# One dealt list for the first group of a linear-attention kernel with a feed-forward block behind it

## The chip, the cores and the metric

The kernel runs on one core of a Trainium2 chip. Its engines are TensorE (PE; PEld is its weight load), VectorE (DVE), ScalarE (ACT), GpSimd (POOL) and SyncE (SP), which here issues nearly all DMAs. Each engine takes its instructions strictly in the order in which the program lists them, and waits at the head of its list for semaphores of the others. The metric is the time of one execution in microseconds, the median of several runs.

## The reference

For every batch and head (4 x 8) a state of 40 x 40 is carried through 768 steps, and the result of all heads (3072 rows of 320) goes through a feed-forward block with a gate.

```python
for t in range(S):
    y[:, :, t] = einsum('bhd,bhde->bhe', rt, state)
    Sa = einsum('bhde,bhe->bhd', state, at)
    state = state * wt - einsum('bhd,bhe->bhde', Sa, bt) + einsum('bhd,bhe->bhde', vt, kt)
x = y.transpose(0, 2, 1, 3).reshape(B * S, H * D)     # 3072 x 320
h = x @ w_in                                           # 320 x 2048
g = h * clip(h + 3, 0, 6) / 6
out = g @ w_out                                        # 2048 x 320
```

`w_in` and `w_out` arrive as 64-bit floats; the kernel makes 32-bit floats of them itself.

## The kernel before

The 768 steps are cut into blocks of 64, two at a time for two batches: 24 units, and four units (0 to 3) are a group. A unit has preparation stages (`W` and `gam`: running products of the decay by scans; `A`, `B`, `K`: transposes and scaling; `F`: the matrix to be inverted; `factor`; `E`, `EV`), and solving stages (`RT`, `VT`, `C`, `R`, `U`, `UT`, `S`, `rS`, `sn`, `H`, `y`, `move`). Between the two stands, once per group, the inversion of the group's 32 x 32 triangles, `invert` (L776): two transposes on DVE around 60 small steps, a product (L803) and a sum (L809) in turn, and then two third blocks, X and Y (`third_block`, L829), on PE and ACT, which make `tinv`. Units 0 and 2 share one state, units 1 and 3 the other. Unit 2's `R` needs the state after unit 0's `sn`.

The weights are converted in 20 pieces by the generator `load_weights` (L305). A piece is four steps: an AND on DVE with two Prelu activations on ACT behind it (L354, L355, L357), the product that finishes the piece before (L365), an AND/OR (L374), and a multiply-add (L378). The raw pieces are fetched by SP (L332) into space that is free for the moment. The 13th uses the space of the tile `x` (`raw_x`), the 14th that of `fb` (`raw_fb`), the 15th that of `tt` (`raw_tt`), both left over from the inversion; the 16th and 17th are called `raw` again. How many may be issued at all is `limit`; the token `@` in the list opens it to all 20.

The order of the instructions is written out by hand, since pools and schedule are manual. `run` lets a stage go to its next end, `aside(n)` takes n inversion steps, `deal(n)` takes n steps of the weight conversion, `fetch` (L477) has SP load an input (the stage `RT` of unit 1, 2 or 3 asks for the next unit's `R`, all of them into one tile, so that the load waits until that tile has been read), and `pieces(n)` takes n pieces of the feed-forward stream (`expand`, L1169: products `h` with `win`; `contract`, L1210: products `o` with `wout`). In the first group four lists stand one behind another: `FIRST` (preparation up to `F`), `BESIDE` (the rest of the preparation, one inversion step between stages), a loop over the remaining inversion steps with `STEPS` (at which of them a conversion step is taken, and seven early stages at every fifth), and `PLAN` (solving stages, conversion steps, feed-forward pieces, and `&`, which takes a step of the second group). From the token `&` on the same program follows for the other five groups: PE gets feed-forward pieces between the stages of units 4 to 23.

Of the kernel before, what the change touches and what calls it, by code (L numbers as in the profile page):

```python
# [12 lines left out]
AF = mybir.ActivationFunctionType  # L13
# [3 lines left out]
P = 128  # L17
BL = 64
HB = BL // 2
L = 32  # L20
# [11 lines left out]
def kernel(  # L32
# [42 lines left out]
    nc = tc.nc  # L75
    B, H, T, D = r.shape
# [3 lines left out]
    NU = 2 * NP  # L80
    DM, DFF = moe_w_in.shape
    NJ = DFF // P
    NH = NU * H
# [57 lines left out]
    def ps_pair(*dims):  # L141
# [21 lines left out]
        out=ident[:], in_=ones, pattern=[[1, P]],  # L163
# [4 lines left out]
        out=ones[:, 0:BL], in_=ones[:, 0:BL], pattern=[[1, BL]],  # L168
# [3 lines left out]
        out=ones[BL:P, 0:BL], in_=ones[BL:P, BL:P], pattern=[[1, BL]],  # L172
# [5 lines left out]
    three = const.tile([P, 1], F32, name="three")  # L178
# [59 lines left out]
    tinv = const.tile([P, NH, BL], F32, name="tinv")  # L238
# [24 lines left out]
    for i, (x, y) in enumerate([(0, DFF // 2), (0, NJ // 2)]):  # L263
        for n, z in enumerate((x, y)):
# [4 lines left out]
            name = ("WA", "BK")[i][n]  # L269
# [8 lines left out]
    converted = [0]  # L278
    phase = [0]
    limit, refill = [2], []  # L280
# [155 lines left out]
    def blocked(name, i):  # L436

        return i >= {"A": 3 * NU, "R": 2 * NU}.get(name, NK)
# [41 lines left out]
    def fetch(name, i, engine=None):  # L480

        if i is None or i >= NK:
            return
        x, crossed = {"W": (w, 0), "A": (a, 0), "B": (b, 0), "K": (k, 0), "R": (r, 1),
                      "V": (v, 1)}[name]
        if name == "V":
            t = values[i % AHEAD]
        else:
            t = placed.get((name, i))
            if (name, i) == ("R", 1):  # L490
                t = others["K"]
            t = t if t is not None else (others if i < 2 * NU and i % 2 and name != "R" else inputs)[name]
        g, p = names[i]
        if blocked(name, i):
            t = fetch_blocks(name, x, 2 * p, g, i == (2 * NU if crossed else 3 * NU))
            data[i][name + "N"] = t
            return
        engines = engine or nc.sync
        for q in range(2):
            engine = engines[q] if isinstance(engines, tuple) else engines  # L500
            y = x[2 * p + q, :, g * BL:(g + 1) * BL, :]
            rows = slice(q * BL, (q + 1) * BL)
            if crossed:
                for s in range(2):
                    engine.dma_start(out=t[rows, 4 * s:4 * s + 4, 0:D],  # L505
                                     in_=y[s::2].rearrange("h t e -> t h e"))
            else:
                engine.dma_start(out=t[rows, :, 0:D], in_=y.rearrange("h t e -> t h e"))  # L508
        data[i][name + "N"] = t
# [254 lines left out]
    def in_turn(stages, order):  # L764

        for name in order:
            yield from stages[name]()
            shared[0] = None
            yield DONE
# [107 lines left out]
    def third_blocks(first=False):  # L877

        zs = inv.tile([P, 2, 2, H, L], F32, name="zs", tag="x", bufs=1)
        return [third_block(*third[-1], 2 * n, zs[:, n], first) for n in range(2)]  # L880
# [359 lines left out]
    weights = load_weights()  # L1240
# [11 lines left out]
    def aside(n, weight=0):  # L1252

        for _ in range(n):
            if side and next(side[0], side) is side:
                side.popleft()
            due[0] += weight
            while due[0] >= 1:
                due[0] -= 1
                next(weights, None)  # L1260

    def deal(n):

        for _ in range(n):
            next(weights, None)

    def run(stage, steps=0, mixed=0, deals=0):

        for at in stage:
            if at == DONE:  # L1270
                return
            aside(steps, mixed)
            deal(deals)

    third, F, group_F = [], None, []

    def prepared(i):
        nonlocal F
        if i >= NK:
            return None  # L1280
        if i % NU == 0:
            F = inv.tile([P, NH, BL], F32, name="F", tag="F", bufs=2)
            group_F.append(F)
        return prepare(i, F)
# [3 lines left out]
    EARLY, MIXED, MOVED = 5, 0.27, 2  # L1288
# [23 lines left out]
    begin = [prepared(i) for i in range(NU)]  # L1312
    for group, first in ("WAB", 0), ("WAB", 2), ("K", 0), ("V", 0), ("K", 2), ("V", 2):
        if (group, first) == ("V", 2):
            next(weights)
        for name in group:
            for i in range(first, first + 2):
                fetch(name, i, (nc.sync, nc.scalar) if first == 0 and name != "V" else None)
    FIRST = "0W 1W 0gam 1gam 0A 1A 2W 3W 0B 1B 0F 1F 2gam 3gam 2A 3A 2B 3B 2F 3F".split()
    BESIDE = "2K 1K 1factor 0K 3K 0factor 2factor 0E 3factor 1E 2E 0EV 3E 3EV 2EV 1EV".split()  # L1320
    chains = [in_turn(begin[i], [x[1:] for x in FIRST + BESIDE if x[0] == str(i)]) for i in range(NU)]
    for x in FIRST:
        run(chains[int(x[0])])
# [3 lines left out]
                        (SLOT, 6 * D, SLOT + 8, L), (SLOT, 6 * D + BL, SLOT + 8, L)):  # L1327
        nc.gpsimd.tensor_copy(select[x:x + D, at:at + n], ident[x:x + D, c:c + n])
    side.append(invert(group_F[-1], third, True))
    for n, x in enumerate(BESIDE):  # L1330
        limit[0] = {0: 4, 8: 12}.get(n, limit[0])
        while n == 0 and refill[0]():
            pass
        if n == 4:
            fetch("R", 0)
            fetch("R", 1)
        run(chains[int(x[0])], 1, MIXED if n >= 12 else 0)
    TURNS_IN = [("one", 1), ("pair", 2), ("pair", 2)]
    blocks = {}


    stages = [step(i) for i in range(NU)]
    chains = [in_turn(stages[0], ["RT", "VT", "C", "R"]), in_turn(stages[1], ["RT", "VT", "C"])]
    early = deque(chains[i] for i in (0, 0, 1, 1, 0, 1, 0))
    STEPS = (4, 12, 13, 27, 29, 31, 35, 37, 55, 58, 62, 64, 67)
    n, cleared = 0, []
    while not third:
        aside(1)
        if not third:
            n += 1  # L1350
            if n in STEPS:
                next(weights, None)
            if converted[0] >= 2 and not cleared:
                cleared.append(True)
                for z in range(0, P, BL):
                    nc.scalar.activation(out=tinv[z + L:z + BL, :, 0:L], func=AF.Copy, scale=0.0,
                                         in_=_ap(three[z + L:z + BL], 0, [[0, NH], [0, L]]))
            if n % EARLY == 0 and early:
                run(early.popleft())
    assert not early and cleared  # L1360
    limit[0] = 13
    while phase[0] == 1:
        next(weights)
    firsts = third_blocks(True)

    def block(i, j):

        if i % NU < 2:
            if j == 0:
# [3 lines left out]

    PLAN = """X:2 X 0U:4 +1 0UT:1 0sn:2 1R 0H:1 1U 1UT:2
              0y 1sn:1 0move:1 Y:2 2RT:1 1H:1 Y:1 2VT:3 1y:2 2R
              2S:3 2U:3 1move:1 3RT:2 ! @ 2UT 2C:3 2rS:3 3R:4
              *2 3VT 3S:1 2sn:3 *1.5 2H:6 *3 3U:1 # 3UT:7
              2y:3 +8 +1 +2 +2 +1 +1 +3 +1 +2  # L1380
              +2 +4 3C:6 +1 +4 +2 +3 +3 +3 +2
              +5 +4 +3 +1 +2 +4 +1 +5 & +1
              +4 +2 +3 +4 +1 +3 +4 3rS:13 +5 +2
              +1 +3 +3 +4 +3 +3 3sn +2 +4 +1
              +1 +2 +1 +2 +2 +2 +1 +1 3H:8 +4
              +4 & +2 +6 +1 +1 +1 +6 +3 +1
              +3 +4 +2 +6 +4 % +3 +1 +3 +2
              +1 +2 +2 +1 +3 *2.5 +4 2move:8 *1.5 +2
              +1 +3 +2 & +2 +3 2move2:17 +5 3y:4 +4
              & +1 +3 3move:5 +1 +3 +1 +3 +2 +1  # L1390
              +2 +1 +4 & +3 3move2:1 +4 +2 & +2
              +2 +3 +2 +4"""
    chains = {str(i): in_turn(stages[i], [x[1:].split(":")[0] for x in PLAN.split() if x[0] == str(i)])
              for i in range(NU)}
    chains.update({x: firsts[n] for n, x in enumerate("XY")})
    for x in PLAN.split():
        if x == "!":
            begun_ffn()
            ring.clear()
            ring.extend([("one", 1), ("whole", 2)])  # L1400
        elif x == "@":
            limit[0] = PIECES
        elif x == "#":
            seconds()
            for name in "WA":
                fetch(name, NU + 1)
            third.clear()
            second_group = by_twos(NU, 3, 0, 1.25)
        elif x == "%":
            for name in "BK":  # L1410
                others[name] = second(name)
                fetch(name, NU + 1)
        elif x == "&":
            next(second_group)
        elif x[0] == "*":
            pieces(float(x[1:]))
        elif x[0] == "+":
            deal(int(x))
        else:
            name, *amounts = x.split(":")  # L1420
            run(chains[name[0]], 0, 0, *map(int, amounts))
    for _ in weights:
        pass
    for _ in second_group:
# [94 lines left out]
    m = 0  # L1519
# [54 lines left out]
```

## Time and profile before

| what | us |
|---|---|
| median of 3 runs (786.43, 787.64, 795.53) | 787.64 |
| profiled execution, as timed | 790.31 |
| its span in the profile | 788.6 |
| PE busy in the span (91%) | 721.2 |
| DVE busy (64%) | 506.9 |
| ACT busy (38%) | 299.9 |
| POOL busy (21%) | 168.9 |
| mean granted clock of TensorE, share of full speed | 0.954 |

The span is one execution as the hardware profiler saw it; 1.7 us of the timed 790.31 lie around it. Busy shares are averages over the whole span. In a timeline row the first number is the start in the span, the second the length; then follow engine, line, operation, and what is written from what. A wait is put down to the instruction that came last before the waiting one could go.

### The profile page before, as it was taken

The page shows a single profiled execution, that of the slowest core. Times are in us where ns is not written, and L with a number is a line of the kernel's source. Part 1 is how long each engine was busy: PE and PEld are TensorE (multiplying, and loading weights), DVE is VectorE, ACT ScalarE, POOL GpSimd, SP SyncE. Part 2 cuts the span into 40 slices and gives each one's busy share as a digit, 9 for nine tenths or more (in the row PEclk, how much of TensorE's full clock was granted, in tenths as well). Part 3 has the DMA queues.
Part 4 walks back from the last instruction along what each step waited for, and adds up shares of the span by engine and source line. Part 5 has one row for each costly group of instructions (what it writes and reads, how often), then busy time and mean ns, then how long its engine had stood idle before and what let it go on. Part 6 is the DMA issues. An engine that isn't in the chain of part 4 may idle for free.

```text
span 788.6 us, 32724 instructions
## 1 busy us (share of the span) xinstructions
PE 721.2 (91%) x14456; PEld 610.9 (77%) x14456; DVE 506.9 (64%) x1018; ACT 299.9 (38%) x634; POOL 168.9 (21%) x319
## 2 busy tenths in 40 slices
PE   5736968999899898999999999999999999999998
PEld 3625757878779786888788878888888888888886
DVE  7898869789455799455899355997635982233110
ACT  2345853321554442443324454134543242422111
POOL 7503002420232412122203222203212120000000
PEclk9755789999999999899999999999999999999999
DMA  9672374330233431343322343313332101111000
GB/s 124 120 199 83 75 194 73 66 56 9 52 72 71 89 69 29 69 87 80 66 58 48 66 83 84 75 35 68 72 71 57 38 18 45 41 38 28 20 9 17
DMA packets 195698, 52.34 MB, mean 66 GB/s; under 512 B 179428, under 2 KB 194276, under 8 KB 195556
## 3 DMA queue, kind: packets, MB, share of 16 engines
q1 hardware_dynamic: 187932, 46.88, 30.0%
q10 hardware_dynamic: 7624, 3.36, 1.7%
q8 instruction: 114, 1.87, 1.0%
q14 instruction: 28, 0.23, 0.1%
HBM read 38.67 MB, written 3.93 MB: 54 GB/s over the span
## 4 chain that ended last, share of the span: by engine, by line
PE 72%; DVE 12%; ACT 4%; issue 4%; SPq 3%; DMA 3%; ACTq 1%; POOL 0%; DVEq 0%; POOLq 0%
PE h L1169 26%; PE o L1210 23%; PE pair L562 4%; PE pair L1043 3%; DVE x L809 2%; DVE prod L803 2%; PE pair L534 2%; SPq L508 2%; PE pair L961 2%; PE one L524 1%; PE pair L981 1%; PE pair L997 1%; PE pair L921 1%; PE pair L861 1%; SPq L505 1%
## 5 line engine op out<-in xcount | busy, mean ns | idle before, releaser
L1169 PE MATMUL h<-xt,win 128*128 128x128 f32 (+1 forms) x2304 | 249.7, 283 | 2.6 <-DVE gt L1185 2.6
L1169 PEld LDWEIGHTS h<-xt,win 128*128 128x128 f32 (+1 forms) x2304 | 231.0, 192 | 18.7 <-DVE gt L1185 3.3
L1210 PE MATMUL o<-wout,gt 128*128 128x320 f32 x768 | 227.3, 441 | 0.0
L1210 PEld LDWEIGHTS o<-wout,gt 128*128 128x128 f32 x768 | 138.9, 190 | 51.6
L1185 DVE SCALAR_TENSOR_TENSOR gt<-gt,h 128x512 f32<-128x512 f32 x96 | 61.9, 682 | 103.0 <-ACT gt L1184 102.8
L1184 ACT ACTIVATE gt<-h,three 128x512 f32<-128x512 f32 x96 | 62.0, 685 | 120.9 <-PE h L1169 101.6
L809 DVE TENSOR_TENSOR x<-x,prod 128x30 f32<-128x30 f32 (+9 forms) x180 | 65.1, 361 | 5.8
L803 DVE TENSOR_TENSOR prod<-x 128x30 f32<-128x30 f32 (+9 forms) x180 | 64.6, 359 | 6.5 <-POOL x L788 1.3
L575 DVE COPY_PREDICATED store<-mask,pair 128x512 f32<-128x512 int32 x40 | 29.2, 731 | 53.1 <-PE pair L562 37.8
L723 POOL TENSOR_TENSOR KBt<-K,rgt 128x320 f32<-128x320 f32 x19 | 16.6, 872 | 163.7 <-ACT rgt L712 163.6
L1051 POOL TENSOR_TENSOR yg<-ys,gam 128x512 f32<-128x512 f32 x20 | 25.4, 1270 | 115.9 <-DVE ys L1050 84.2
L599 DVE TENSOR_TENSOR_SCAN prods<-wm,start 128x528 f32<-128x528 f32 x24 | 33.5, 1402 | 12.2 <-ACT wm L596 11.8
L1043 PE MATMUL pair<-store,KBt 64*64 64x104 f32 x1280 | 32.6, 250 | 0.7 <-ACT F L693 0.5
L757 ACT ACTIVATE EV<-pair 64x320 f32<-64x320 f32 x44 | 18.9, 431 | 37.0 <-PE pair L752 33.5
L610 DVE TENSOR_TENSOR_SCAN wm<-wm,start 128x528 f32<-128x528 f32 x24 | 31.0, 1291 | 0.8
L1043 PEld LDWEIGHTS pair<-store,KBt 64*64 64x64 f32 x1280 | 29.2, 133 | 1.4 <-ACT F L693 0.7
L738 DVE TENSOR_TENSOR kt<-pair,rgam 128x512 f32<-128x512 f32 x15 | 10.3, 685 | 30.0 <-PE pair L703 29.6
L642 POOL TENSOR_TENSOR at<-at,gam 128x512 f32<-128x512 f32 x12 | 15.3, 1272 | 57.7 <-DVE at L478 51.9
L1228 ACT ACTIVATE ob<-o 128x320 f32<-128x320 f32 x22 | 9.6, 437 | 46.0 <-issue 26.3
L965 ACT ACTIVATE store<-pair 128x320 f32<-128x320 f32 x23 | 10.0, 435 | 42.2 <-PE pair L981 31.5
L950 ACT ACTIVATE S<-pair 128x512 f32<-128x512 f32 x16 | 9.6, 597 | 43.4 <-DVE store L575 23.6
L871 ACT ACTIVATE tinv<-pair 32x256 f32<-32x256 f32 x48 | 17.9, 373 | 16.4 <-PE pair L861 13.3
(306 smaller groups left out, 1069.9 us busy)
## 6 DMA issues: line engine op xcount, KB each, us to landing
R<-in_r_dram SPq DMA_DIRECT2D x156, 40.0 KB
A<-in_a_dram SPq DMA_DIRECT2D x61, 80.0 KB
V<-in_v_dram SPq DMA_DIRECT2D x96, 40.0 KB
out_dram<-ob SPq DMA_DIRECT2D x47, 80.0 KB
B<-in_b_dram SPq DMA_DIRECT2D x42, 80.0 KB
store<-V SPq DMA_DIRECT2D x20, 160.0 KB
W<-in_w_dram SPq DMA_DIRECT2D x37, 80.0 KB
K<-in_k_dram SPq DMA_DIRECT2D x37, 80.0 KB
```

The costliest lines, as they stand in the source:

```text
L562: nc.tensor.matmul(out=o[i][half(q), n, :], lhsT=lhs[half(i, D), n ^ (2 * q * swap), half(q)], rhs=rhs[half(i, D), n ^ (2 * q * back), hal ...
L575: nc.vector.copy_predicated(out=x[:, :, 0:BL].rearrange("p (h i) t -> p i h t", i=2), mask=mask8, data=o[2])
L599: nc.vector.tensor_tensor_scan(out=prods[:].rearrange("p r m i -> p (r m i)"), data0=wm[:, 0:SCAN], data1=start[:], initial=0.0, op0=ALU.m ...
L610: nc.vector.tensor_tensor_scan(out=back, data0=back, data1=start[:], initial=0.0, op0=ALU.mult, op1=ALU.add)
L803: nc.vector.tensor_tensor(out=pv, in0=_ap(x[:], (i + 1) * L + i, [[L, n], [0, i]]), in1=_ap(x[:], i * L, [[0, n], [1, i]]), op=ALU.mult,)
L809: nc.vector.tensor_tensor(out=rest, in0=rest, in1=pv, op=ALU.add)
L1043: nc.tensor.matmul(out=y[q][half(s), pr, :], lhsT=o[name][half(q), h * D:h * D + SLOT], rhs=m[name][half(q), x, :], start=(name == "K" and ...
L1051: nc.gpsimd.tensor_tensor(out=yg[:], in0=m["ys"][:].rearrange("p r q t -> p r (q t)"), in1=o["G"][:], op=ALU.mult)
L1169: nc.tensor.matmul(out=hp[c][:, i, :], lhsT=lhsT, rhs=rhs, start=(begun[c] == 0), stop=(begun[c] == 3 * NQ - 1))
L1184: nc.scalar.activation(out=gt[:], in_=hp[c][:], func=AF.Relu, bias=three[:], scale=1.0)
L1185: nc.vector.scalar_tensor_tensor(out=gt[:], in0=gt[:], scalar=6.0, in1=hp[c][:], op0=ALU.min, op1=ALU.mult)
L1210: nc.tensor.matmul(out=op[:], lhsT=gts[c][:, n, :], rhs=wout[:, c * HJ + r * NQ + n, :], start=((split or r == 0) and c == 0 and n == 0), ...
```

## The change

The three lists behind `FIRST` become one `PLAN`, and some orders in it are new. New tokens: `i` or `m` behind a stage's number takes an inversion step at its inner stop (`m` with a share of a conversion step), `=n` takes n inversion steps, `Ln` sets `limit`, `<` fetches raw pieces, `r` fetches `R` of units 0 and 1, `z` clears a part of `tinv`, `T` takes what is left of the inversion and makes X and Y. `+n`, `*n`, `!`, `@`, `#`, `%` and `&` are what they were, and the feed-forward pieces in the list add up to 10.5 in both.

```diff
-    FIRST = "0W 1W 0gam 1gam 0A 1A 2W 3W 0B 1B 0F 1F 2gam 3gam 2A 3A 2B 3B 2F 3F".split()
-    BESIDE = "2K 1K 1factor 0K 3K 0factor 2factor 0E 3factor 1E 2E 0EV 3E 3EV 2EV 1EV".split()
+    FIRST = "0W 0gam 1W 1gam 0A 1A 2W 3W 0B 1B 0F 1F 2gam 3gam 2A 2B 3A 3B 2F 3F".split()
+    BESIDE = "0K 1K 1factor 0factor 2K 2factor 0E 3K 2E 3factor 1E 0EV 2EV 1EV 3E 3EV".split()
...
-    for n, x in enumerate(BESIDE):
...
-        run(chains[int(x[0])], 1, MIXED if n >= 12 else 0)
...
-    early = deque(chains[i] for i in (0, 0, 1, 1, 0, 1, 0))
-    STEPS = (4, 12, 13, 27, 29, 31, 35, 37, 55, 58, 62, 64, 67)
-    while not third:
-        aside(1)
...
-    PLAN = """X:2 X 0U:4 +1 0UT:1 0sn:2 1R 0H:1 1U 1UT:2
-              0y 1sn:1 0move:1 Y:2 2RT:1 1H:1 Y:1 2VT:3 1y:2 2R
-              2S:3 2U:3 1move:1 3RT:2 ! @ 2UT 2C:3 2rS:3 3R:4
-              *2 3VT 3S:1 2sn:3 *1.5 2H:6 *3 3U:1 # 3UT:7
-              2y:3 +8 +1 +2 +2 +1 +1 +3 +1 +2
-              +2 +4 3C:6 +1 +4 +2 +3 +3 +3 +2
-              +5 +4 +3 +1 +2 +4 +1 +5 & +1
...
+    PLAN = """1K:0i L4 < 1factor:0i r 0K:0i 0factor:0i 2K:0m 2factor:0i 0E:0i
+              3K:0i 2E:0i =1 1E:0i 2EV:0m 1EV:0m =5 L12 3factor:0i =4
+              0EV:0i 3E:0m 3EV:0m 0RT =2 +1 =1 =4 +1 0VT
+              =4 =4 =1 1RT =1 +1 +1 =2 +1 =3
+              1VT +1 =4 0C +1 =1 =2 1C =1 =1
+              +1 =2 +1 z =4 =2 =2 =11 =1 +1
+              T 0R:1 X X:2 0U:4 0UT 0sn:2 1R:2 +1 1U
+              0H:1 1UT:2 1sn:1 0y 2RT:1 Y:2 0move:1 1H:1 Y:1 2VT:3
+              1y:1 2R 2S:4 @ 1move 3RT:2 2U:3 ! 2UT 2C:3
+              *1.5 2rS:3 3R:4 3VT:1 # *2 2sn:2 3S:1 2H:6 *3
+              3U:1 3UT:7 2y:4 +1 3C:3 +2 & 3rS:11 3sn:1 *2.5
+              3H:8 & % *1.5 2move:6 & 2move2:15 3y:4 & 3move:4
+              & 3move2:3 &"""
...
+        elif x == "T":
+            while not third:
+                aside(1)
+            limit[0] = max(13, limit[0])
+            while phase[0] == 1:
+                next(weights)
+            chains.update({x: x_chain for x, x_chain in zip("XY", third_blocks(True))})
+        elif x[0] == "=":
+            for _ in range(int(x[1:])):
+                if not third:
+                    aside(1)
```

Instruction by instruction, none is added or taken away. On PE, DVE, ACT and POOL the two programs differ in order up to the beginning of the second group only, and so do SP's loads.

More of the change, by code (lines that the diff above doesn't have):

```diff
@@ L1329 @@
     side.append(invert(group_F[-1], third, True))
-    for n, x in enumerate(BESIDE):
[L1331 to L1336, printed above, removed]
-        run(chains[int(x[0])], 1, MIXED if n >= 12 else 0)
     TURNS_IN = [("one", 1), ("pair", 2), ("pair", 2)]
     blocks = {}
-    stages = [step(i) for i in range(NU)]
-    chains = [in_turn(stages[0], ["RT", "VT", "C", "R"]), in_turn(stages[1], ["RT", "VT", "C"])]
-    early = deque(chains[i] for i in (0, 0, 1, 1, 0, 1, 0))
-    STEPS = (4, 12, 13, 27, 29, 31, 35, 37, 55, 58, 62, 64, 67)
-    n, cleared = 0, []
-    while not third:
-        aside(1)
[L1349 to L1364, printed above, removed]
+    stages = [{**begin[i], **step(i)} for i in range(NU)]
     def block(i, j):
@@ L1372, in block @@
             run(blocks[i])
-    PLAN = """X:2 X 0U:4 +1 0UT:1 0sn:2 1R 0H:1 1U 1UT:2
-              0y 1sn:1 0move:1 Y:2 2RT:1 1H:1 Y:1 2VT:3 1y:2 2R
-              2S:3 2U:3 1move:1 3RT:2 ! @ 2UT 2C:3 2rS:3 3R:4
-              *2 3VT 3S:1 2sn:3 *1.5 2H:6 *3 3U:1 # 3UT:7
-              2y:3 +8 +1 +2 +2 +1 +1 +3 +1 +2
-              +2 +4 3C:6 +1 +4 +2 +3 +3 +3 +2
-              +5 +4 +3 +1 +2 +4 +1 +5 & +1
[L1383 to L1392, printed above, removed]
+    PLAN = """1K:0i L4 < 1factor:0i r 0K:0i 0factor:0i 2K:0m 2factor:0i 0E:0i
[7 more added lines that the diff above has]
+              1y:1 2R 2S:4 @ 1move 3RT:2 2U:3 ! 2UT 2C:3
+              *1.5 2rS:3 3R:4 3VT:1 # *2 2sn:2 3S:1 2H:6 *3
+              3U:1 3UT:7 2y:4 +1 3C:3 +2 & 3rS:11 3sn:1 *2.5
+              3H:8 & % *1.5 2move:6 & 2move2:15 3y:4 & 3move:4
+              & 3move2:3 &"""
     chains = {str(i): in_turn(stages[i], [x[1:].split(":")[0] for x in PLAN.split() if x[0] == str(i)])
               for i in range(NU)}
-    chains.update({x: firsts[n] for n, x in enumerate("XY")})
     for x in PLAN.split():
@@ L1400 @@
             ring.extend([("one", 1), ("whole", 2)])
+        elif x[0] == "L":
+            limit[0] = int(x[1:])
+        elif x == "<":
+            while refill[0]():
+                pass
+        elif x == "r":
+            fetch("R", 0)
+            fetch("R", 1)
+        elif x == "z":
+            assert converted[0] >= 2
+            for z in range(0, P, BL):
+                nc.scalar.activation(out=tinv[z + L:z + BL, :, 0:L], func=AF.Copy, scale=0.0,
+                                     in_=_ap(three[z + L:z + BL], 0, [[0, NH], [0, L]]))
+        elif x == "T":
[9 more added lines that the diff above has]
+                    aside(1)
         elif x == "@":
@@ L1420 @@
             name, *amounts = x.split(":")
-            run(chains[name[0]], 0, 0, *map(int, amounts))
+            between = amounts[0][-1] if amounts and amounts[0][-1] in "im" else ""
+            deals = int(amounts[0].rstrip("im")) if amounts else 0
+            run(chains[name[0]], int(between != ""), MIXED if between == "m" else 0, deals)
     for _ in weights:
```

## The prediction

> **What bounds it now.** I began with the page: engines, then the forty slices (19.7 us each).
>
> ```profile
> PE 721.2 (91%) x14456; PEld 610.9 (77%) x14456; DVE 506.9 (64%) x1018; ACT 299.9 (38%) x634; POOL 168.9 (21%) x319
> ...
> PE   5736968999899898999999999999999999999998
> ...
> DVE  7898869789455799455899355997635982233110
> ...
> PEclk9755789999999999899999999999999999999999
> ```
>
> From the seventh slice on PE is busy eight to nine tenths or more at nearly full clock: the feed-forward products fill it, its order there stays, and what comes earlier shifts all of it. PE idles most in the first six slices, some 120 us (45 of them), and there DVE is the fullest engine. That is where the change works. Its instructions are the same in number, so no term below is work; each is a wait or an order. Next came the waits of DVE and of PE, 60 to 126 us (us in total, times, longest):
>
> ```profile
> DVE parts L354 <- DMA raw_fb<-in_moe_w_in_dram: 4.5, 1, 4.5
> DVE gt L1185 <- ACT gt L1184: 2.2, 1, 2.2
> DVE yg L1073 <- PE lent L1065: 2.1, 1, 2.1
> DVE yg L1073 <- PE pair L1065: 1.6, 1, 1.6
> ```
>
> ```profile
> PE pair L1015 <- DVE RR L925: 5.0, 1, 5.0
> ```
>
> One cause stands behind the largest wait on both engines. DVE reaches the AND of the 14th raw piece at 99.2 and gets it at 103.7; unit 3's `RR` (L925) stands two instructions behind it, and PE's `sn` of unit 2 (L1015) needs the bank that this empties. Why the piece is late, SP's timeline tells (start, length):
>
> ```profile
> 83.69 1.90 SPq L332 DMA_DIRECT2D raw_x<-in_moe_w_in_dram  x2
> 85.64 11.54 SPq L505 DMA_DIRECT2D R<-in_r_dram  x8
> 97.22 1.06 SPq L332 DMA_DIRECT2D raw_fb<-in_moe_w_in_dram  x2
> 98.32 2.98 SPq L332 DMA_DIRECT2D raw_tt<-in_moe_w_in_dram  x4
> ```
>
> Eight loads of `R` are issued in 11.5 us, where eight of `V` take 6.1 (row at 16.24). Four are unit 3's; the other four, unit 4's, wait for PE to read unit 3's tile, transposed from 93.5 to 94.4. `raw_fb` stands behind them in SP's list, while nothing moves (GB/s is the last column):
>
> ```profile
> 90.00:95.00 5.00, 4.99 (x76) 4.24 (x72) 4.79 (x11) 4.57 (x8) 0.00 (x0) 0.60 0.00 2
> 95.00:100.00 5.00, 4.70 (x120) 4.34 (x120) 4.14 (x9) 3.86 (x6) 0.00 (x0) 1.00 0.53 123
> 100.00:105.00 5.00, 0.21 (x2) 0.00 (x0) 1.31 (x3) 0.81 (x2) 0.17 (x1) 0.93 0.91 244
> 105.00:110.00 5.00, 4.82 (x104) 4.52 (x104) 4.93 (x11) 3.90 (x7) 0.28 (x2) 0.50 0.59 175
> ```
>
> PE's five empty microseconds (first column pair) are followed by five at clock 0.50 (third from the end).
>
> **The parts.**
>
> *Preparation (`FIRST`).* DVE idles 0.8 us at 7.6 for ACT's `wm` of unit 1. In the new order unit 0's L608 and L610 fill that, but ACT now copies unit 0's `gam` and `rgam` ahead of `wm`: two copies end some 0.75 us after L610, then `wm` takes 0.67, so DVE idles about 1.4 before unit 1's scan. Unit 0's `at` starts at 13.55 instead of 13.28. Later unit 2's `bt` goes ahead of unit 3's `at`, so that the first `F` product is done while DVE makes the rest, and only unit 3's product (0.9) and its copy (0.6) stand behind the last `bt`. That gives back up to 0.3. Sum: between -0.3 and +1.4 (nothing given back), taken as 0, since two independent shifts of 0.3 stand against each other.
>
> *Beside the inversion.* From 26 to 64 us DVE runs without a gap. Before the end of the inversion it does the same four `kt`, six masks and 60 steps, and one conversion step more, an AND/OR: +0.35 by its pitch (0.34 to 0.45). The stages that change place there are on PE and ACT, both mostly idle: their cover is the inversion itself (PE waits 11.8 us for it). Unit 2's `E` and `EV` now need `V` of unit 2 first; those loads are issued from 28.3 to about 31.5 and stay where they are. The fetch of `R` is asked for sooner, but SP issues back to back until 56 and keeps this order: 0.
>
> *The first third blocks.* ACT's timeline:
>
> ```profile
> 64.69 1.56 ACT L846 ACTIVATE zs<-lent 32x256 f32<-32x256 f32 x4 [3.69 <-DVE tt L817]
> 67.39 1.56 ACT L871 ACTIVATE tinv<-pair 32x256 f32<-32x256 f32 x4 [1.15 <-PE pair L861]
> 68.97 0.72 ACT L355 ACTIVATE parts<-parts,low 128x512 f32<-128x512 int32 x1
> 69.73 0.72 ACT L357 ACTIVATE parts<-parts,low 128x512 int32<-128x512 f32 x1
> 70.47 0.44 ACT L965 ACTIVATE store<-pair 128x320 f32<-128x320 f32 x1
> 70.81 0.71 ACT L355 ACTIVATE parts<-parts,low 128x512 f32<-128x512 int32 x1
> 71.55 0.72 ACT L357 ACTIVATE parts<-parts,low 128x512 int32<-128x512 f32 x1
> 72.18 0.58 ACT L987 ACTIVATE UT<-lent 128x512 f32<-128x512 f32 x1
> ```
>
> A pair of activations (1.45) moves into the gap of 1.15 ahead of L871, which is then some 0.3 late, and none stands between L965 and L987 any more (1.37). L965 comes about 0.2 later, `UT` 0.8 sooner: -0.8 + 0.35 = about -0.4 for `UT`.
>
> *Stages of units 1 to 3.* Now unit 1's `U` stands ahead of unit 0's `H` on PE (it waits for `RR`, 0.46 behind `UT` on ACT; a product at half clock is 1.1), unit 0's `y` behind unit 1's `sn`, and `move` of unit 0 behind Y's first product. `y` and `move` come 2 us later; they lead to `xt`, which PE first needs at 97. On the other side Y's first product stands at 80 in both, and `xt` of unit 0 and a conversion pair no longer share ACT with its copies in the old order: `tinv` is complete 0.7 sooner. Unit 2's `U`, which stood ahead of `move` of unit 1 (3.0 at low clock) and unit 3's `RT` (0.9), stands behind both. Before, its result was held on ACT from 90.8 to 93.7 by `S` and four conversion activations, so that the new place costs the path little: PE reaches `rS` of unit 2 at about 95.6 (now 95.7). DVE saves its wait for `y` of unit 1 (2.1) in part. Walked through by rows, DVE comes to the AND of the 14th piece at about 98.2 instead of 99.2. Bounds: +2 (all of `y`'s delay on the path) and -3 (both `yg` waits, 3.7, less the 0.35 and 0.3 above); I take -1.
>
> *`@` ahead of unit 3's `RT`.* It opens the last seven pieces before the load of unit 4's `R` is listed. SP can then issue `raw_fb` behind unit 3's `R`, at about 88.3 instead of 97.2, and `raw_tt` behind it. By its old times (issued 97.2, used 103.7) it has landed by 94.9, ahead of 98.2: the wait of 4.5 goes. Behind it in SP's list are `raw_tt` (before: 98.3 to use 106.2, 7.9 us; after: 89.4 to 100.5), then the first `raw`; the second `raw` now waits behind unit 4's `R`, issued at about 97 and used at 108: 11 us, where 102 to 114.8 was enough. Unit 4's `R` itself is used only in the second group. `#` ahead puts the loads of `W` and `A` before the 18th and 19th piece; 2.6 us of issue (four at 0.65), against 9.5 us between issue and use of `raw_fb`'s second piece: hidden; uncovered it would cost 2.6. If the 14th piece landed late all the same, the whole 4.5 would stay. Taken: -4.5.
>
> *After it.* With the gap gone, PE's `sn` follows its `h` products with no half clock, and DVE's 2.2 us for `gt` (L1185) shrinks, as PE finishes `h` sooner. From 0 to -3 (2.2 of `gt`, and half of the 1.5 that PE then waits for it); I take -1. The feed-forward pieces, 10.5 in sum, only change places.
>
> [...] The row is the clock 0.50 from 105 to 110 behind an idle 5.0. [...]
>
> **Sum.** 0 + 0 (the 0.35 is in the -1) - 1 - 4.5 - 1 = -6.5 at the start of the second group. I keep -6, since later waits of PE from 125 to 330 us (2.7, 1.8, 1.6 and less) may take up some. The profiled execution goes from 790.3 to 784.3; the median of the runs, 787.64, is 2.7 below that one, so the forecast is 781.6.
>
> **Rivals.** *Part is taken back* (chance 0.2): another wait is late next, such as DVE's for `sn` and `H` of unit 2, whose `U` now stands behind two stages. For it: three of the four waits above are of DVE for PE. Against: unit 2's `U` had been held on ACT anyway. Gain 4.5 + 1 - 3.5 = 2: 785.6.
>
> *PE sets the pace* (0.08): the clock stays up from 95 on, the `gt` waits vanish, and both `yg` waits: 4.5 + 3 + 3 = 10.5: 777.1. [...] Against it is DVE's row at 105, full.
>
> *Slower: unit 2's `U` waits for a load* (0.1). It used to be independent of unit 3's `R`; now it is queued on PE behind its transposes, and with it `UT`, `sn`, `H`. That `R` is issued behind `raw_x`, which waits for Y's last product to read `x`'s space. PE comes to the transposes at about 91.5; the loads end their issue at 88.2 and an `R` load lands in 2 to 3 us (2.25 at 246.67). If Y slips, each microsecond beyond 1 is a wait. A slip of 6 outweighs the gain, and at 8 it is 2 slower than before: 789.6. Against: Y comes at 80 by my walk.
>
> *It doesn't do what it says* (0.02): SP's list could keep `raw_fb` behind the `R` loads. In the built lists it stands ahead of unit 4's.
>
> **How the numbers follow.** The forecast has 0.6 (776 to 785). The range leaves out about 2 in 10: from 777 (-10.5, the fast rival's end) to 789 (+1.4, the preparation's upper bound with nothing gained, most of the slow rival outside). Two per cent is 15.8 us, about what a measurement can tell from no change. Faster by that would need more than all bounds together (3 + 4.5 + 3): 0.02. Slower by it would need a slip of Y by 22: 0.03. Within: 0.95.
>
> **What would show it.** `raw_fb` issued near 88, no wait of L354 for it, no PE gap near 100 and no clock of 0.5 behind it; `UT` near 71.8; the first `W` transposes of the second group near 113 instead of 119.9, and the rest shifted as a block. A wait of PE for `R` near 91, or of DVE for L1015 or L562 near 100, would prove me wrong; so would a shift at 120 that is gone by 200.

## The result, and the profile after

| 22 runs each | median us | lowest to highest |
|---|---|---|
| before | 787.78 | 783.1 to 796.51 |
| changed | 784.40 | 779.0 to 788.55 |

The ratio is 0.9956 (95% interval 0.9936 to 0.9976): a small gain that is there, 3.4 us by the medians, far inside the 2% that count as the same. The profiled execution took 784.76 us (span 783.0), 5.55 less than that of before.

The engines and the forty slices (19.6 us each) of the changed kernel's page:

```profile
PE 720.2 (92%) x14456; PEld 608.6 (78%) x14456; DVE 507.0 (65%) x1018; ACT 300.0 (38%) x634; POOL 169.8 (22%) x319
...
PE   5745879999899998999999999999999999999998
...
DVE  7898798688446798445998455996635982323110
...
PEclk9855899999999998899999999999999999999999
```

Busy times are the same to 1 us (PEld, which overlaps PE, to 2.3). In the sixth and seventh slice (98 to 137 us) PE's digits go from 6, 8 to 7, 9, and in the fifth and sixth its clock's from 7, 8 to 8, 9.

SP's timeline of the changed kernel shows the one moved load that the prediction counted on (start, length):

```profile
84.21 3.20 SPq L505 DMA_DIRECT2D R<-in_r_dram  x4
87.51 1.01 SPq L332 DMA_DIRECT2D raw_fb<-in_moe_w_in_dram  x2
88.57 3.17 SPq L332 DMA_DIRECT2D raw_tt<-in_moe_w_in_dram  x4
91.83 0.39 SPq L332 DMA_DIRECT2D raw<-in_moe_w_out_dram  x1
93.12 3.24 SPq L505 DMA_DIRECT2D R<-in_r_dram  x4
```

The eight loads of `R` are now two times four, and `raw_fb` goes between them at 87.51 instead of 97.22. DVE's timeline at that piece:

```profile
99.01 0.69 DVE L378 SCALAR_TENSOR_TENSOR raw_x<-raw_x 128x512 f32<-128x512 uint32 x1
99.62 0.42 DVE L354 TENSOR_SCALAR parts<-raw_fb 128x512 uint32<-128x512 uint32 x1
...
100.56 0.48 DVE L925 TENSOR_TENSOR RR<-pair,EV 128x320 f32<-128x320 f32 x1
```

No row carries an idle time in brackets: the AND of the 14th piece starts when DVE comes to it. What is left in the waits from 60 to 126 us (us in total, times, longest):

```profile
DVE yg L1073 <- PE lent L1065: 3.7, 2, 2.7
...
DVE state L1022 <- PE pair L1015: 1.6, 1, 1.6
```

The 4.5 for `raw_fb`, the 2.2 for `gt` and PE's 5.0 for `RR` are gone. Both waits for `y` are still there, 3.7 as before. The windows in which PE had stood still for five microseconds:

```profile
90.00:95.00 5.00, 4.40 (x78) 3.72 (x76) 4.90 (x11) 3.99 (x7) 0.00 (x0) 0.73 0.89 244
95.00:100.00 5.00, 4.37 (x118) 4.14 (x119) 4.88 (x12) 4.29 (x8) 0.00 (x0) 1.00 0.58 148
100.00:105.00 5.00, 4.51 (x120) 3.92 (x120) 4.93 (x12) 3.90 (x8) 0.45 (x2) 1.00 0.44 74
105.00:110.00 5.00, 3.00 (x88) 2.68 (x86) 4.93 (x10) 3.77 (x6) 0.00 (x0) 1.00 0.71 209
```

The column of the clock (third from the end) reads 1.00 from 95 on, and DVE (third pair) is busy 4.88 to 4.93 of 5: behind the 14th piece DVE sets the pace now, without a break. The first `W` transposes of the second group come at 113.44 instead of 119.87. I call this place W below; it is the mark by which the first group can be compared apart from all that follows.

### The profile page after: what moved, and what is told of

It reads as the page before. It is cut to its first block, busy times and chain, and to the rows that moved or that the text cites. A ratio compares the mean times of both kernels' runs of the same rounds, so it can differ in the third digit from the quotient of the medians.

```text
span 783.0 us, 32729 instructions
## 1 busy us (share of the span) xinstructions
PE 720.2 (92%) x14456; PEld 608.6 (78%) x14456; DVE 507.0 (65%) x1018; ACT 300.0 (38%) x634; POOL 169.8 (22%) x319
## 4 chain that ended last, share of the span: by engine, by line
PE 72%; DVE 13%; issue 4%; SPq 4%; ACT 3%; DMA 3%; POOL 0%; ACTq 0%; DVEq 0%; POOLq 0%
PE h L1169 26%; PE o L1210 23%; PE pair L562 4%; PE pair L1043 3%; PE pair L534 2%; SPq L508 2%; DVE x L809 2%; DVE prod L803 2%; PE pair L961 1%; PE pair L752 1%; PE one L524 1%; PE pair L921 1%; PE pair L997 1%; PE pair L981 1%; SPq L505 1%
## 5 line engine op out<-in xcount | busy, mean ns | idle before, releaser
L809 DVE TENSOR_TENSOR x<-x,prod 128x30 f32<-128x30 f32 (+9 forms) x180 | 65.9, 366 | 6.0
L562 PE MATMUL pair<-RT,VT 40*64 40x64 f32 x768 | 18.2, 236 | 7.6 <-ACT VT L932 3.6
```

The costliest lines, as they stand in the source:

```text
L562: nc.tensor.matmul(out=o[i][half(q), n, :], lhsT=lhs[half(i, D), n ^ (2 * q * swap), half(q)], rhs=rhs[half(i, D), n ^ (2 * q * back), hal ...
L809: nc.vector.tensor_tensor(out=rest, in0=rest, in1=pv, op=ALU.add)
```

## The experiments

Two theories stood against each other: that the place of `@`, which changes nothing but SP's list, carries the gain; and that the new dealing of steps and stages carries it. All kernels compute everything. Every time stands beside runs of the kernel before on the same chip.

| kernel | median us | before there | ratio, 95% interval | W |
|---|---|---|---|---|
| before (two traces) | | | | 119.87, 119.99 |
| changed (three traces) | 784.40 / 784.84 / 784.06 | 787.78 / 790.81 / 790.43 | 0.9956 / 0.9934 / 0.9927 | 113.44, 113.13, 112.66 |
| e1_at | 785.86 | 791.04 | 0.9947 (0.9910 to 0.9984) | 112.58 |
| e2_noat | 786.97 | 791.04 | 0.9945 (0.9915 to 0.9975) | 115.42 |
| e5_tail | 793.20 | 791.04 | 1.0032 (1.0002 to 1.0062) | 120.62 |
| e6_front | 794.73 | 791.04 | 1.0045 (1.0023 to 1.0067) | 119.81 |
| e7_tail_phase | 785.48 | 790.81 | 0.9945 (0.9920 to 0.9971) | 112.41 |
| e8_y | 784.71 | 790.81 | 0.9941 (0.9914 to 0.9967) | 112.24 |
| e9_fill | 784.87 | 789.69 | 0.9947 (0.9922 to 0.9972) | 112.35 |
| e10_afterfill | 782.15 | 789.69 | 0.9909 (0.9878 to 0.9940) | 113.54 |
| e11_fill_later | 783.60 | 790.43 | 0.9924 (0.9895 to 0.9953) | 112.81 |

### `@` alone, and everything but `@`

e1_at is the kernel before with one token moved:

```diff
-              2S:3 2U:3 1move:1 3RT:2 ! @ 2UT 2C:3 2rS:3 3R:4
+              2S:3 @ 2U:3 1move:1 3RT:2 ! 2UT 2C:3 2rS:3 3R:4
```

> The kernel before with one token moved: the permission for the last seven raw pieces stands ahead of unit 2's U instead of behind unit 3's RT, so that the 14th piece's loads are listed ahead of unit 4's R on SP. The other engines keep their lists. If that order is what the gain is made of (theory 1): no wait of DVE for the 14th piece (4.5 us before), no 5.0 us gap of PE near 100, the first W transposes of the second group 4 to 5 us sooner than 119.9, and 3 to 4.5 us faster in time. If the other moves of the dealt list carry it (theory 2): the wait goes, but another takes its place; W moves by under 1.5 us and the time by under 1 us.

Measured: `raw_fb` issued at 88.43, its AND at 98.47 without a wait, W at 112.58: 7.3 us sooner than in before (4 to 5 were expected), as much as the whole change reaches in the best of its three traces. The time is 0.9947 of before. One moved token in SP's list is enough for all of the gain.

e2_noat is the changed kernel with that token put back:

```diff
-              1y:1 2R 2S:4 @ 1move 3RT:2 2U:3 ! 2UT 2C:3
+              1y:1 2R 2S:4 1move 3RT:2 @ 2U:3 ! 2UT 2C:3
```

> The changed kernel with the same token put back behind unit 3's RT; only SP's list differs from the changed kernel. Theory 1: the 14th piece is issued near 96 again, DVE waits 3.5 to 5 us for it, and 3 to 5 us of the gain are lost, so that the time is within 1 us of the kernel before. Theory 2: at most 1.5 us are lost, it stays 2 us or more faster than before.

Measured: the loads are back in the old order, but the wait is not. SP's timeline and, below it, DVE's in that kernel:

```profile
84.23 10.95 SPq L505 DMA_DIRECT2D R<-in_r_dram  x8
95.24 1.06 SPq L332 DMA_DIRECT2D raw_fb<-in_moe_w_in_dram  x2
```

```profile
99.93 0.43 DVE L354 TENSOR_SCALAR parts<-raw_fb 128x512 uint32<-128x512 uint32 x1 [1.22 <-DMA raw_fb<-in_moe_w_in_dram]
```

`raw_fb` is issued 2 us sooner than in before, is there 4.7 us later (6.5 in before: 97.22 to 103.69), and the wait is 1.2, with 0.7 more for `raw_tt`, instead of 4.5. W comes at 115.42. So in the old list the early `@` is sufficient, and in the new one it is not necessary. Without it the new list still brings 4.45 at W; with it, 2 more. Why `raw_fb` is issued sooner can be read in the list, where unit 3's `RT`, which frees the tile of `R`, now stands ahead of unit 2's `U`: its transposes (L524) start at 91.40 instead of 93.50. Why `raw_fb` lands faster stays open.

### The two halves

e5_tail has the lists of before up to the end of the inversion, and the changed `PLAN` behind it; e6_front the other way round.

```diff
-    PLAN = """X:2 X 0U:4 +1 0UT:1 0sn:2 1R 0H:1 1U 1UT:2
+    PLAN = """X X:2 0U:4 0UT 0sn:2 1R:2 +1 1U
...
```

> The three lists up to the end of the inversion as they were before; the solving list behind it as changed. In the changed kernel the inversion ends 0.95 us later than before (61.8 against 60.8). Theory 1: this part costs what it is late, so that here the inversion ends near 60.8 again, W stands 0.5 to 1 us sooner than the changed kernel's 113.4, and the time is 0.3 to 1 us better than the changed kernel's, 4 to 4.5 us under before. Rival: the conversion step taken early in the front pays for its lateness; then W is no sooner than 113.4.

```diff
-              T 0R:1 X X:2 0U:4 0UT 0sn:2 1R:2 +1 1U
+              T 0R:1 X:2 X 0U:4 +1 0UT:1 0sn:2 1R 0H:1 1U 1UT:2
...
```

> The complement: the front as changed, the solving list as before, with the 14th piece behind unit 4's R. Theory 1: the wait for the 14th piece stays (3 to 5 us), the inversion ends 0.95 us later, W stands at 119.5 to 121, the time is 0 to 1 us above before. Rival (the front carries a part of the gain): 1 us or more under before.

Measured: neither half gains; both are slower than before, 1.0032 and 1.0045, with both intervals clear of 1. For e5_tail both forecasts failed. `raw_fb` is issued at 87.02 and there is no wait for it, and W is at 120.62 all the same: with the early `@` in place the gain can still be lost. The inversion (L812), which was to end near 60.8 again, ended at 61.73. In e6_front, which has the late `@`, W is at 119.81, as forecast, but the time is 3.7 us above before and not 0 to 1, the wait for `raw_fb` is 1.15 and not 3 to 5, and PE's wait L861 for `zs` is 5.3 us (1.9 in before). What the halves have in common is that the conversion steps, which both lists count on from wherever the front left them, stand two places off the stages that they were dealt between. In before and in the changed kernel 19 conversion steps come on DVE ahead of unit 0's `sn` (L1022); in e5_tail it is 17, in e6_front 21.

### Two steps

e7_tail_phase tests that. It is e5_tail with two conversion steps more behind the inversion (`+1`, and one more inside `X`), so that 19 come ahead of unit 0's `sn` again and every engine's order from there on is that of the changed kernel:

```diff
-    PLAN = """X X:2 0U:4 0UT 0sn:2 1R:2 +1 1U
+    PLAN = """+1 X X:3 0U:4 0UT 0sn:2 1R:2 +1 1U
```

> Like the tail alone (front as before, solving list as changed), but with one conversion step taken at once behind the inversion and one more in X, so that every engine's list behind the inversion is the changed kernel's. If the tail alone was slow only because its conversion steps fell one step off their places: W of the second group near 113.4 (120.6 without the step), time 0.993 to 0.998 of before. If the changed front is needed for something else (early state, fetches, clock): it stays at 1.000 or above and W at 117 or later.

Measured: W at 112.41 instead of 120.62, ratio 0.9945 instead of 1.0032. The expectation speaks of one step; the lists differ by two. An AND/OR and a multiply-add (L374, 0.42, and L378, 0.69) that DVE takes ahead of `sn` instead of behind it, with all later steps two places sooner, are worth 8 us. The windows of e5_tail (us; busy PE, PEld, DVE, ACT, POOL; clock, DMA share, GB/s):

```profile
76.00:90.00 14.00, 12.01 (x436) 10.65 (x428) 9.74 (x19) 10.54 (x20) 0.00 (x0) 0.74 0.57 142
90.00:105.00 15.00, 12.25 (x206) 11.20 (x204) 12.95 (x27) 10.00 (x18) 0.62 (x2) 0.73 0.56 140
105.00:121.00 16.00, 11.93 (x299) 10.67 (x299) 12.10 (x24) 9.17 (x15) 0.00 (x0) 0.77 0.47 121
```

and those of e7_tail_phase:

```profile
76.00:90.00 14.00, 11.02 (x443) 9.70 (x432) 11.46 (x23) 10.85 (x22) 0.00 (x0) 1.00 0.57 137
90.00:105.00 15.00, 11.86 (x317) 10.13 (x315) 14.59 (x31) 12.81 (x22) 0.45 (x2) 1.00 0.80 182
105.00:113.00 8.00, 4.63 (x173) 4.17 (x174) 7.90 (x16) 6.48 (x11) 0.00 (x0) 1.00 0.58 171
```

PE's clock is about three quarters in all windows of the one and full in all of the other. DVE, which has the most to do here, is busy 12.95 and 12.10 in the one, 14.59 of 15 and 7.90 of 8 in the other: at the low clock it waits for PE at `sn` (L1022, 4.4 us instead of 2.0), at `yg` and at L571, and PE waits for it in turn. How much of the 8 us the waits cost by themselves, and how much the low clock, these two runs don't separate. They do show that the front of the change (`FIRST`, `BESIDE` and the steps of the inversion) gives nothing: with the old front and the fitting steps, W is as early as in the changed kernel. It is so although the inversion ended at 62.40 in e7_tail_phase, later than in any other trace here: how early the inversion ends does not decide W.

### The waits for `y`

The waits for `y` of units 0 and 1 had outlived the change. e8_y is e1_at with a conversion step moved ahead of the first, and two ahead of the second; only DVE's order differs from e1_at.

```diff
-              0y 1sn:1 0move:1 Y:2 2RT:1 1H:1 Y:1 2VT:3 1y:2 2R
-              2S:3 @ 2U:3 1move:1 3RT:2 ! 2UT 2C:3 2rS:3 3R:4
+              0y:1 1sn 0move:1 Y:2 2RT:1 1H:1 Y:1 2VT:3 1y:4 2R
+              2S:1 @ 2U:3 1move:1 3RT:2 ! 2UT 2C:3 2rS:3 3R:4
```

> The kernel with the moved token alone, and on DVE one conversion step ahead of each of the two products of unit 0's and unit 1's y; no other engine's list changes. If DVE's waits for y (1.7 and 1.3 us there) are on the path: they shrink by 1 us or more together, W stands near 111.8 instead of 112.6, and it is 0.5 to 1 us faster than the kernel with the token alone, the fastest of all. Rival: PE's wait behind y sets the end anyway, and RR of unit 2, later on DVE by the step, costs what is gained: no change within 0.5 us.

(The expectation counts one step for each `y`.) Measured: the waits shrink from 3.0 (1.7 and 1.3 in e1_at) to 1.2, and W comes only 0.3 sooner, at 112.24, which is less than the traces of one unaltered program differ by (113.44, 113.13, 112.66). DVE's waits for PE at L1022 grow from 0.3 to 1.1 at the same time. So most of a removed wait is late at the next one; my 3.7 of `yg` waits were never worth 3.7. The ratio, 0.9941, can't be told from those of e1_at and of the changed kernel, though its profiled span was 778.6, the shortest of all.

### The same program twice

That span asked how far one trace carries. So both kernels were profiled again unaltered.

> The kernel before once more, unaltered, for the same comparison. The order on SP makes the 14th piece late again: DVE waits 3 to 5 us for it and PE 3 to 5 us near 100. If that wait is as short as in the changed kernel with the token put back (1.2), the 4.5 us were chance and not the order.

> The changed kernel once more, unaltered, to see what differs between two executions of one program. [...] Time 0.994 to 0.998 of before.

Measured: before took 790.48 (span 788.8 against 788.6) and shows the wait for `raw_fb` again, 4.7. The changed kernel took 784.84 as median and 785.6 in its profiled run. In the two traces of the changed kernel the start of the second group agrees within 0.3 us, but not what follows: from the end of the third group's inversion (L812) to the sum of its `y` (L1050) the one takes 29.62 us, the other 28.74. The kernels above take 26.8 (e2, e8), 26.9 (e5), 28.6 (e6), 29.0 (e7) and 29.5 (e1) for the same instructions. PE stands still for 2.6 us at L838 in that stretch in all of them, and then has a stretch of half clock of changing length (3.4 to 10.2 us). That is a third theory, about the part behind the change: what happens to a shift of 6 us on its way to the end would be decided by how the clock falls behind such gaps.

### Filling the gap behind

To fill that gap, e10_afterfill moves two feed-forward pieces in the changed kernel, e9_fill the same two in e8_y (the digits are pieces between blocks of the other groups, the second list those of them that come first, the third inversion steps beside each):

```diff
-    GAPS = "71042423221267761421...
-    FIRSTS = "50021102120130201200...
-    INVERSION = "01210000000015231100...
+    GAPS = "71042423221267743421...
+    FIRSTS = "50021102120130203200...
+    INVERSION = "01210000000015241100...
```

> The changed kernel with one thing moved, behind the first group: two feed-forward pieces (1.16 us each on PE) of the 16th place between blocks go to the 17th, ahead of the third group's third blocks (L838), where PE waits 2.6 us for the end of the inversion; of 18 inversion steps dealt beside them 16 stay and 2 move with the pieces. Clock theory (the 2.6 us idle lets the clock fall, and which window it falls in decides how long the stretch behind it takes): the idle of L838 near 305 goes to under 1 us, no window between 300 and 330 has a clock under 0.9, the same work from the end of the inversion (L812 of the third group) to L1050 takes 26.5 to 27.5 us instead of 28.7 and 29.6 in two traces of the changed kernel, and the time is 1.5 to 2.5 us less: 782.5 to 783.5, 0.2 to 0.3% under the changed kernel. Rival (DVE and the inversion set the pace there, the clock only follows): the idle stays as long because the inversion ends 2 us later, or moves to the place that gave the pieces up; clock and time as before, 784.8.

> The same two pieces moved in the kernel that has of the change only the place of `@` and one conversion step ahead of the `y` of unit 0 and one of unit 1 (its trace already caught the good phase there: 26.8 us at clock 0.94, span 778.6, while its median was 784.7). Clock theory: its profile gains at most 0.5 us against that trace, its median 1 to 2.5 us, and its runs spread less, since fewer of them fall into a long stretch of half clock. Rival: median 784.7 and the same spread.

Measured: the gap stays at 2.68 us in both. My design was wrong: the two pieces had stood ahead of the gap already, so that PE had no more to do there than before. That it is a window that decides how long the half clock lasts was my guess; no run here shows it. The stretch takes 26.95 and 26.83. e9_fill has the median of e8_y, 784.87; e10_afterfill has the lowest of all, 782.15, but I found nothing in its trace that explains it, and its interval overlaps those of the unaltered changed kernel.

e11_fill_later takes the two pieces from behind the gap instead. DVE's, POOL's and SP's orders are those of the changed kernel, which ran beside it on the same chip.

```diff
-    GAPS = "71042423221267761421...
-    FIRSTS = "50021102120130201200...
+    GAPS = "71042423221267763311...
+    FIRSTS = "50021102120130203200...
```

> The changed kernel; two `h` pieces (1.16 us each on PE) that stood behind the third group's first third block (L838) are done ahead of it, where PE waits 2.62 us for DVE; the two pieces before this one had been moved from ahead of the same wait and could not fill it. DVE's, POOL's and SP's lists are the same. Clock theory: the idle ahead of L838 shrinks to 0.3 to 0.5 us, no window between 305 and 335 has a clock under 0.9 (0.50 and 0.71 at 310 and 315 in the trace of the changed kernel), from the end of the inversion (L812 of the third group) to L1050 goes from 29.6 and 28.7 to 25.5 to 27 us, and the time from 784.8 to 782 to 783, beside the same kernel unaltered on the same chip 0.997. Rival: the stretch is set by DVE, or L861 and L871 now wait in place of L838, and length and time stay: 784.8, 1.000.

> The changed kernel unaltered, for the comparison with the one run beside it: 784.8. By the clock theory its trace has the idle of 2.6 us ahead of L838 near 305 and at least one window of clock 0.85 or less within 10 us behind it, but takes anything from 26.8 to 29.6 us from the end of the inversion to L1050, as the same program did before (29.6 and 28.7).

Measured: the gap ahead of L838 on PE's timeline (idle time in brackets), first in the first trace of the changed kernel, and then its windows from 305 to 320,

```profile
307.89 1.08 PE L838 MATMUL pair<-tb,F 32*32 32x32 f32 x64 [2.62 <-DVE state L1055]
```

```profile
305.00:310.00 5.00, 2.38 (x77) 2.15 (x77) 4.84 (x10) 2.70 (x8) 2.98 (x6) 0.77 0.30 65
310.00:315.00 5.00, 5.00 (x96) 4.80 (x95) 3.17 (x10) 1.19 (x3) 0.34 (x2) 0.50 0.43 91
315.00:320.00 5.00, 5.00 (x87) 4.52 (x86) 1.09 (x2) 1.45 (x4) 1.32 (x2) 0.71 0.35 80
```

then the same windows of the same program in its third trace, where the gap is again 2.62,

```profile
305.00:310.00 5.00, 2.85 (x84) 2.82 (x86) 4.88 (x8) 2.57 (x8) 2.68 (x5) 0.75 0.34 76
310.00:315.00 5.00, 5.00 (x164) 4.67 (x161) 3.56 (x9) 0.79 (x2) 0.99 (x1) 0.91 0.40 85
315.00:320.00 5.00, 5.00 (x144) 4.08 (x143) 1.28 (x2) 4.42 (x11) 0.34 (x2) 1.00 0.36 82
```

and e11_fill_later:

```profile
308.21 0.74 PE L838 MATMUL pair<-tb,F 32*32 32x32 f32 x64 [0.85 <-DVE state L1055]
```

```profile
305.00:310.00 5.00, 4.15 (x102) 3.80 (x100) 4.86 (x9) 3.03 (x8) 2.98 (x5) 1.00 0.25 58
310.00:315.00 5.00, 4.55 (x158) 3.82 (x156) 4.57 (x11) 1.72 (x4) 1.41 (x4) 1.00 0.48 101
315.00:320.00 5.00, 4.75 (x149) 3.65 (x138) 1.28 (x2) 3.58 (x10) 0.59 (x2) 1.00 0.37 82
```

With 2.62 of idle the same program gets 0.50 and 0.71 once, and 0.91 and 1.00 another time. With 0.85 the clock stays at 1.00. The stretch to L1050 takes 29.62, 28.74 and 26.81 us in the three traces of the changed kernel, and 25.93 in e11_fill_later. That half of the theory holds. The other half, that the time falls by 2 to 3 us, does not: 783.60 against 784.06 beside it, 0.9924 and 0.9927 of before. Half a microsecond is less than the medians of the unaltered changed kernel differ by (784.06 to 784.84), so these runs show no gain from this one place.

## Why the prediction was right, and where it was not

**The place of `@`, -4.5: right, in each detail.** Issue at 88.3 forecast, 87.5 measured; the wait of L354 gone, PE's 5.0 at L1015 gone, `raw_tt` and the later pieces covered. The runs add that the old order costs what it costs only in the old list: e2_noat pays 1.9 for it. The prediction put the term down to one edit; it belongs to the order of `R`, `raw_fb` and DVE's list together.

**Preparation, 0: right.** DVE's wait for `wm` is 1.19 (forecast 1.4), and the end of `FIRST`, L783, comes at 26.05 instead of 26.19.

**Beside the inversion, +0.35: too small.** It ended 0.95 later (61.80 against 60.84). The conversion step more is there. What I had not seen is unit 3's `KBt` on POOL, which comes later in the new order and beside other instructions. POOL's timeline and DVE's, of the changed kernel:

```profile
39.03 1.79 POOL L723 TENSOR_TENSOR KBt<-wout,rgt 128x320 f32<-128x320 f32 x2 [3.76 <-ACT rgt L715]
```

```profile
38.72 0.37 DVE L803 TENSOR_TENSOR prod<-x 128x198 f32<-128x198 f32 x1
39.12 0.99 DVE L809 TENSOR_TENSOR x<-x,prod 128x198 f32<-128x198 f32 x1
40.14 0.92 DVE L803 TENSOR_TENSOR prod<-x 128x210 f32<-128x210 f32 x1
41.09 0.38 DVE L809 TENSOR_TENSOR x<-x,prod 128x210 f32<-128x210 f32 x1
```

Two steps that take 0.36 and 0.38 in before (at 40.80 and 41.19) take 0.99 and 0.92 here. In before that `KBt` ran from 35.37 to 37.10, beside a mask (L571, 0.73, as long as elsewhere) and two smaller steps, of which one was stretched (L809, 0.83 at 36.42). Over the inversion the sixty steps add up to 22.9 us instead of 22.3. In these rows the two steps beside `KBt` are stretched to about the length of one of POOL's two instructions (1.79 for both); why they are, no run here shows.

**First third blocks, `UT` at 71.8: 72.16.** That is 0.36 later than forecast, less than the inversion's extra 0.6, and 0.02 ahead of before.

**The walk through units 1 to 3, -1: wrong.** DVE came to the AND of the 14th piece at 99.62, 0.45 later than before; the other two traces of the changed kernel have 99.31 and 98.84, against 99.17 and 99.29 in the two of before: about where it was. Both `yg` waits stayed (3.7), where I had let the second one shrink in part, and 0.6 of the miss is the inversion. The step of the walk that failed is the one on `y` and `move` of unit 0: they come 2 us later and lead to `xt`, "which PE first needs at 97". PE needs it at 83.3. ACT comes to that `xt` (L1095) at 83.89 instead of 80.95, now behind the copies of Y's first product (L846) and a pair of conversion activations, and PE's transposes of unit 2's `V` wait until it has read its bank. PE's timeline, of before and of the changed kernel:

```profile
83.55 0.94 PE L524 MATMUL pair<-ident,V 128*128 128x128 f32 x4
```

```profile
84.44 0.66 PE L524 MATMUL pair<-ident,V 128*128 128x128 f32 x4 [1.13 <-ACT xt L1095]
```

This wait, 1.13 in all three traces of the changed kernel, is in no trace with the old order of these stages. Behind it L1065 starts at 85.02 instead of 84.41 and stops for 1.49 in its own issue (1.10 in before), and DVE's longest wait for `y` grew from 2.1 to 2.7. The clock was no worse than in before (the row from 85 to 90 reads 0.58, and 0.50 in before). In e7_tail_phase, with the same order, the same wait (1.16) and that row at 1.00, DVE comes to the AND at 98.31, 0.9 sooner than before. So about the -1 shows up where the clock is full, which I had not counted on; how the rest splits between the wait, the inversion and the clock stays open.

**After it, -1: too small.** From that AND to W it is 16.18 us in before and 13.82 in the changed kernel: -2.4. The 2.2 of `gt` vanished whole, and PE's half clock with it (from 105 to 110 it was 0.50 in before and is 1.00 in the changed kernel).

**The sum at W, -6.5: 113.44 against 119.87, -6.4.** It is right because the two last errors (+1.45 and -1.4) cancel, which is luck. By its terms the prediction was less good than by its sum.

**Kept to the end, -6, and the median of 781.6: too low by 2.8.** In the profiled executions 5.55, 4.7 and 6.8 us are left, around the forecast 6, but not because 6.5 at W came through as a block. The stretch behind the third group's inversion (28.58 us in before) took 1.0 and 0.2 us of the shift and gave 1.8 in the third trace; from L1050 to the end another 0, 1.1 and 2.3 were lost, and no run here shows to what. What failed in the median is the last step, which took the 2.7 us between the profile of before and its median as a distance that the changed kernel would have too. The median of before was well placed (787.64, and 787.78 in 22 runs); but where a trace falls in the spread of its kernel (783.1 to 796.5) is its own affair, and that of the changed kernel lies only 0.36 above its median. Against before on the same chip the three measurements give 3.4, 6.0 and 6.4 us (the table). The interval of the first is 1.9 to 5.0 us, which leaves 6 out; those of the other two, 2.8 to 7.7 and 3.5 to 8.1, overlap with it and hold 6.

**The rivals.** *Part is taken back* (785.6) is nearest to the first measurement's 3.4 us, but not by its mechanism: nothing was taken back before W. *PE sets the pace* had its condition, full clock from 95 on, yet DVE remained the bound at 4.9 of 5. *Unit 2's `U` waits for a load* did not come about: the three traces of the changed kernel show no wait for `R`, and e7_tail_phase, with the same order there, one of 0.89 that left W early. No rival named what cost most in the halves: that the conversion steps fall out of phase with the stages, at 8 us for two of them.

## What to carry to other kernels

Before a load is moved for its own sake, look at what stands ahead of it in the issuing engine's list and waits for something else; one token there did all that three rewritten lists did. A list that deals small steps between stages has a phase: count from which step it starts, since two steps off cost more (8 us at W) than the whole change brought. Compare such versions at a mark right behind the change, and distrust what a single trace shows 200 us later: behind a gap of 2.6 us on PE, the same stretch of one program took 26.8 us in one trace and 29.6 in another.

## What was not expected of the hardware

**The clock behind one gap differed from run to run, in whole steps.** An idle of 2.62 to 2.65 us on PE was followed by clocks between 0.50 and 1.00 in the next two windows, in one program, and the same stretch took 29.6, 28.7 or 26.8 us. In finer windows the clock is not in between: it is at 0.50 without a break, for 10.2 us in the first trace of the changed kernel, 6.8 in the second and 3.4 in the third, and at 1.00 around it. One window from inside each of the three, in this order:

```profile
307.75:317.90 10.15, 10.01 (x216) 9.55 (x220) 6.44 (x12) 2.10 (x5) 2.67 (x6) 0.50 0.42 91
```

```profile
310.25:316.95 6.70, 6.26 (x99) 5.92 (x96) 4.70 (x11) 1.30 (x3) 1.90 (x4) 0.50 0.43 83
```

```profile
307.55:310.90 3.35, 3.35 (x75) 3.17 (x62) 3.23 (x6) 1.50 (x4) 0.90 (x3) 0.50 0.43 91
```

All thirteen traces with this gap (2.60 to 2.68 us), of whatever kernel, have one of these three lengths, and the length goes with the time of the stretch: 3.4 with 26.8 to 26.95 us (six traces), 6.8 with 28.5 to 29.0 (five), 10.2 with 29.5 and 29.6 (two); e11_fill_later, with none, takes 25.93. Which of the three a run gets stays open. The lengths are about one, two and three times 3.4 us; what sets that step, no run here shows. An idle of 2.60 to 2.68 us was followed by half clock in all thirteen. The 2.8 us between the changed kernel's shortest and longest stretch are 0.36% of its span, at one place; the whole change is worth 0.4 to 0.7%.

**A low clock came back again and again.** In e5_tail and e7_tail_phase the same instructions from 76 us on went at clock 0.73 to 0.77 in the one and at 1.00 in the other, after a difference of two conversion steps in DVE's order. In windows of 5 us from 85 to 120 e5_tail reads 0.50, 0.82, 0.86, 0.50, 0.96, 0.72 and 0.59: the clock recovers and falls again. What brings it down again, no run here shows.

**An issue list that stopped moved nothing.** In before, SP stood behind a load of `R` for several microseconds with the DMA share at 0.00 (90 to 95 us), while the load that DVE needed next stood behind it; e1_at, which lists that load first, issues it at 88.43 instead of 97.22. In the changed kernel the same window has a share of 0.89 and 244 GB/s.
